# Norm gain moved from the activations to the first weights, and one kept product moved to another buffer

## The chip, the core and the metric

The program runs on one core of one Trainium2 chip. Five engines of the core appear in the profile: TensorE (PE, with its weight loads as PEld), VectorE (DVE), ScalarE (ACT), GpSimd (POOL) and SyncE (SP, which here only issues DMAs). Each executes its own instructions in order and waits on semaphores for the others. The metric is device time in microseconds (us) of one execution, the median of several runs. Lower is better.

## What is computed

Eight batches of attention with squared ReLU in place of softmax, 12 heads, 448 tokens and 64 columns a head, followed by a normalised two-layer block with a residual:

```python
scores = scale * np.matmul(q, k.transpose(0, 1, 3, 2))
attn = np.maximum(scores, 0.0) ** 2 / S
x = np.matmul(attn, v)                       # heads side by side: (8, 448, 768)
mu = np.mean(x, axis=-1, keepdims=True)
var = np.mean((x - mu) ** 2, axis=-1, keepdims=True)
xn = (x - mu) / np.sqrt(var + 1e-06) * g_ln
ch = np.maximum(xn @ w_ch1, 0.0) @ w_ch2     # 768 -> 3072 -> 768
out = x + ch
```

The vector g_ln has one number for each of the 768 columns of x, which are the rows of w_ch1. The division by the square root is left to the very end, since ReLU lets a positive factor of a token pass through.

## The kernel before

Batches are taken in pairs ("units"). A batch goes through these steps. Attention: `att_QK` writes scores into one of three PSUM slots (L610), `relu` evacuates them on ACT or DVE (L619, L621), `square` follows on DVE or POOL (L634, L636), and `att_AV` (L676) gives x transposed, columns of the model on partitions. `sum_part` adds the pieces of x on POOL into the fp32 buffer `sum_t` (L767, L769, L770). `center` multiplies that by ones on PE (L861), ACT saves the mean into `sum_t` again (`save`, L874), DVE subtracts it (`sub`, L882, four instructions) into the bf16 tile `xc`, and then `gain` multiplies `xc` by g_ln, in six instructions of 128x448, one for each 128 columns, each on ACT (L889) or DVE (L891). The first product reads `xc` and the weights `w1`, [128, 6, 3072] in bf16.

The first product has two forms. Batches 0 to 2 use plain matmuls (`ffn_1`, L971), six to a tile of 128 hidden columns, evacuated by `h_evac` (L1000 on ACT, L1002 on DVE) from two PSUM banks that take turns. From batch 3 on some groups of four tiles are computed with seven half-size products in place of eight (`ffn_1_product`, L1194). The other tiles of these batches stay plain, partly between the products in a slot of attention (`ffn_1_slot`, L989). The seven are called P1, P2, P6, P5, P7, P3, P4, in this order, on an "x" and a "y" bank. Three of their results are kept as fp32 copies outside PSUM (`keep`, L385 on ACT or L387 on DVE): c1 after P1, c2 after P6, p5 after P5. P7 goes on in the x bank and so waits until c2 has been copied. Another three results are added to a kept one by `add_relu` (L1220): C11 uses c1, C22 uses p5, C12 uses c2. Up to batch 6 the kept copies lie in the two buffers of `o_all`: c2 in the one that the last finished output tile was stored from, c1 and p5 in the other, so that each waits for the store of that buffer (`o_done`). In batch 7 they have buffers of their own.

The second product has the plain form (`ffn_2`, L1524) for five tiles of unit 0 and for one tile of each later unit, and a seven-product form (`ffn_w`, L1433) for the rest. In the plain form an output tile is two halves of 24 matmuls. Each half fills one of the two PSUM banks and is evacuated by one DVE instruction (L1540), which also multiplies by the token's factor from `rstd` (root on ACT, L838, reciprocal on DVE, L840) and adds x. A half needs the bank of the half two before it.

The order on every engine is fixed when the program is recorded: a planner (`Order`) keeps a modelled time for each engine, takes the ready operation that could start first, and writes it out. `R.add(engines, costs, emit, deps, key)` hands it an operation that may run on any of the named engines, and the key breaks ties. `segment` lays the matmuls of attention of the next batch ("visits") between those of the block, and runs "hooks" at given steps. `later(...)` and `now_known(...)` pass on an operation that is not yet recorded when another already needs it. POOL also issues the loads of q, k and v (L423, L442) as DMAs.

The stage that follows the first product of batch 1 matters for one of the edits. Its code is:

```python
segment(f1_steps(1) + f2_steps(0, (4, 5, 6, 3, 2)) + fw_steps(0, [0]), vis, 2, 9000.0,
        hooks=[(K2 // 2, lambda: make_sums(0))] ...
```

Of the kernel before, what the change touches and what calls it, by code (L numbers as in the profile page):

```python
# [202 lines left out]
def kernel(  # L203
# [10 lines left out]
    nc = tc.nc  # L214
# [535 lines left out]
    def sum_part(n):  # L750

        b, pn = divmod(n, NPER)
        if b < 2:
            parts = [(slice(0, S), [xT_of(b)[:, i, :] for i in (pn, pn + NPER)])]
        else:
            t, t_left = xT_of(b)
            parts = [(reg(b), [t[:, :, i, :] for i in (pn, pn + NPER)]),
                     (left(b), [t_left[:, i, :] for i in (pn, pn + NPER)])]
        k = 1 if pn == 0 else 2
        op = ops["x_read", b - 1] if pn == 0 else [ops["sum", n - 1]]  # L760
        for cols, x in parts:
            def add(eng, x=x, cols=cols):
                x0, x1, s0, r_t = *x, sum_t[:, cols], rsum_t[:, cols]
                if len(x0.shape) == 3:
                    s0, r_t = (a.rearrange("p (m c) -> p m c", c=P) for a in (s0, r_t))
                if pn == 0:
                    nc.gpsimd.tensor_add(s0, x0, x1)  # L767
                else:
                    nc.gpsimd.tensor_add(s0, s0, x0)  # L769
                    nc.gpsimd.tensor_add(s0 if pn < SUMMED[b] - 1 else r_t, s0, x1)  # L770
            w = cols.stop - cols.start
            ops["sum", n] = R.add("POOL", (120.0 + 2.03 * w) * k, add, ops["x", n] + op, key=-2.0, port=True)
            op = [ops["sum", n]]
# [76 lines left out]
    def center(b):  # L850
# [44 lines left out]
        if b < 2:  # L895
            for ki in [pn + NPER * h for pn in range(NPER) for h in range(2)]:
                def sub_k(eng, ki=ki):
                    if ki == 0:
                        alloc()
                    nc.vector.tensor_sub(xc[b][:, ki, :], xT_of(b)[:, ki, :], mean_ps[b])  # L900
                s1 = R.add("DVE", 620.0, sub_k, [op], key=-2.0)
                subs.append(s1)
                c_ops.append(R.add(*GAIN_ON, lambda eng, ki=ki: gain(eng, ki), [s1], key=-2.5, port=True))
        else:
            t, t_left = xT_of(b)
            for m in range(4):
                cols = slice(r0 + m * P, r0 + (m + 1) * P) if m < 3 else left(b)
                i = t[:, m] if m < 3 else t_left
                subs.append(R.add("DVE", 130.0 + (P if m < 3 else T) * K1 * 1.04,
                                  lambda eng, cols=cols, i=i: sub(eng, cols, slice(0, K1), i), [sv], key=-2.0))  # L910
            for ki in range(K1):
                c_ops.append(R.add(*GAIN_ON, lambda eng, ki=ki: gain(eng, ki), subs, key=-2.5, port=True))
        if b == 0:
            mean_ps["slot"][:] = [subs[-1]]
        elif b == 1:
# [107 lines left out]
    def h_of(b, a, z):  # L1023
        return [later("h", b, i) for i in range(a, z)]

    LAST_B = B - 1
    G4 = K2 // 4
    SH = S // 2
# [13 lines left out]
    def make_w1_sums(first):  # L1042
# [13 lines left out]
        def add(g, name, where):  # L1056

            def emit(eng):
                a11, a12, a21, a22 = (w1_block(g, r, h) for r in range(2) for h in range(2))
                if name == "S3":  # L1060
                    w1q[g, name] = a21
                    nc.vector.tensor_sub(a21, a11, a21)
                    return
                o = w1q[g, name] = home(*where[:2])
                if name == "S1":
                    nc.vector.tensor_add(o, a21, a22)
                elif name == "S2":
                    nc.vector.tensor_sub(o, w1q[g, "S1"], a11)
                else:
                    nc.vector.tensor_sub(o, a12, w1q[g, "S2"])  # L1070
            deps = list(where[2]) if where else [later("f1_end", b_done)]
            prev = {"S1": None, "S2": "S1", "S4": "S2", "S3": "S1"}[name]
            if prev:
                deps.append(ops["w1q", g, prev])
            ops["w1q", g, name] = R.add("DVE", 520.0, emit, deps, key=6.0, port=True)
# [95 lines left out]
    def ffn_1_product(b, g, name):  # L1171
# [32 lines left out]

        def kept(key):
            if b < LAST_B:
                t = o_all[:, e["o"] if key == "c2" else 1 - e["o"], :S]
            elif key == "c2":
                o = W_BLOCK + 3 * KQ * SH + (g % FLIGHT) * 2 * S
                t = at_all[:, o:o + 2 * S].bitcast(fp32)  # L1210
# [7 lines left out]
        def add_relu(key, row, half, other):  # L1218
            def emit(eng):
                nc.vector._custom_dve(TENSOR_ADD_SAT, out=h_out(row, half), in0=e["ps", bank], in1=kept(other),  # L1220
                                      s0=float("inf"), s1=0.0)
            e[key] = R.add("DVE", 620.0, emit, [op, e[other]], key=-3.0)

        def keep(key):
            def emit(eng):
                copy(eng, kept(key), e["ps", bank])
            free = [later("av_done", b)] if b == LAST_B else o_done[e["o"] if key == "c2" else 1 - e["o"]]
            e[key] = R.add(*EITHER, emit, [op, *free], key=-3.0)
        if name in ("P1", "P6", "P5"):
            keep({"P1": "c1", "P6": "c2", "P5": "p5"}[name])  # L1230
# [512 lines left out]
    with tc.manual_schedule():  # L1743
# [54 lines left out]
        def first_pair():  # L1798
# [1 line left out]
            pair_start(0, 0)  # L1800
        segment(f1_steps(1) + f2_steps(0, (4, 5, 6, 3, 2)) + fw_steps(0, [0]), vis, 2, 9000.0,
                hooks=[(K2 // 2, lambda: make_sums(0))]
                + [(i, next_sum) for i in range(K2 // 2 + 1, K2 + 6 * PARTS, SUM_EVERY)] + [(K2 + 6 * PARTS, lambda: make_sums(1)),
                       (K2 + 8 * PARTS, first_pair)]
                + [(i, next_sum) for i in range(K2 + 6 * PARTS + 1, K2 + 10 * PARTS + 2)])
        for b in range(2, B):
# [61 lines left out]
```

## Time and profile before

Three runs took 518.58, 518.02 and 517.56 us, median 518.02. The profiled execution took 518.0 us as a run, and its span in the trace, first instruction to last, is 516.1 us. The other 1.9 us lie around the span.

| what | in the profile before |
|---|---|
| PE busy | 500.2 us, 97% of the span |
| DVE busy | 397.5 us, 77% |
| ACT busy | 225.4 us, 44% |
| POOL busy | 178.3 us, 35% |
| granted TensorE clock | 1.00 in every stretch of 10 us up to 510 us |
| gain on DVE, L891, 128x448 | 30 instructions, 11.9 us |
| gain on ACT, L889, 128x448 | 18 instructions, 11.0 us |
| subtraction of the mean, L882 | 24 instructions, 20.1 us |
| kept products into `o_all`, L385 and L387 | 28 on ACT, 536 ns each; 8 on DVE, 619 ns each |

The first three batches' boundaries lie near 33 us (first product of batch 0 begins), 62 us (batch 1), 159.7 us (batch 2); batch 3's first product begins at 221 us, batch 5's at 342 us. In a timeline each row gives start, length, engine, line, operation, result and operands with their shape, and in brackets how long the engine had been idle before and what released it. Neighbouring instructions of one kind are merged into a row with a count.

### The profile page before, as it was taken

Reading aid. Unit: us, or ns where it says so; the run is one execution under the profiler, and the core shown is the slowest. Engines: PE = TensorE matmul, PEld = TensorE weight load, DVE = VectorE, ACT = ScalarE, POOL = GpSimd, SP = SyncE. Lnnn points to the kernel's source line nnn. Section 1 sums busy time; section 2 is a strip of 40 time slices with the busy share of each in tenths; the row PEclk is TensorE's granted clock in tenths of the full one; section 3 lists DMA queues with packets and bytes.
Section 4 is the critical chain, followed back from the end, with each engine's and each line's share of the span. In section 5 each row is a group of like instructions: output and inputs, shape, how many; then the busy total and the mean of one; then the engine's idle time right before and its main releaser. Section 6 shows DMA issues by size and latency. Waiting matters only on the chain.

```text
span 516.1 us, 10774 instructions
## 1 busy us (share of the span) xinstructions
PE 500.2 (97%) x4416; PEld 305.8 (59%) x4416; DVE 397.5 (77%) x751; ACT 225.4 (44%) x356; POOL 178.3 (35%) x205
## 2 busy tenths in 40 slices
PE   4899999999999999999999999999999999999997
PEld 3444455555554545667556775567655675579864
DVE  5988647847978879778778698885889688976843
ACT  5977622422303564255541565236641476125300
POOL 7420500425633066427543076232266023200000
PEclk9999999999999999999999999999999999999999
DMA  9999999789998178598288676894779620123022
GB/s 192 195 187 196 199 198 144 72 110 111 106 139 102 36 72 89 116 142 86 36 108 104 114 70 67 124 127 56 71 79 142 114 35 1 46 60 50 2 62 61
DMA packets 145948, 51.88 MB, mean 101 GB/s; under 512 B 123238, under 2 KB 144108, under 8 KB 145900
## 3 DMA queue, kind: packets, MB, share of 16 engines
q0 software_dynamic: 82224, 25.50, 46.8%
q1 hardware_dynamic: 59036, 18.82, 21.9%
q10 hardware_dynamic: 4640, 6.88, 4.6%
q8 instruction: 34, 0.56, 0.4%
q14 instruction: 14, 0.11, 0.1%
HBM read 51.91 MB, written 11.01 MB: 122 GB/s over the span
## 4 chain that ended last, share of the span: by engine, by line
PE 91%; DVE 5%; DMA 2%; ACT 1%; issue 1%; DVEq 0%; ACTq 0%
PE f_ps L1433 25%; PE f_ps L971 19%; PE f_ps L1524 12%; PE f_ps L1194 10%; PE sc L610 7%; PE ps L989 6%; PE ps L676 6%; PE x_ps L1194 2%; PE y_ps L1194 2%; DVE at_all L634 1%; DMA out_dram<-o_all 1%; DVE t L387 1%; DMA f<-in_q_dram 1%; DVE a L891 1%; ACT at_all L619 1%
## 5 line engine op out<-in xcount | busy, mean ns | idle before, releaser
L619 ACT ACTIVATE at_all<-sc 128x896 bf16<-128x896 f32 x120 | 105.4, 924 | 78.8 <-PE sc L610 75.8
L971 PE MATMUL f_ps<-a,w 128*128 128x448 bf16 x516 | 102.0, 353 | 1.2 <-DVE h L1002 0.8
L634 DVE TENSOR_TENSOR at_all<-at_all 128x896 bf16<-128x896 bf16 x154 | 96.8, 660 | 1.9 <-ACT at_all L619 1.9
L1433 PEld LDWEIGHTS <-h 128*128 128x128 bf16 x708 | 68.4, 98 | 47.3 <-issue 2.8
L442 POOL DMA_DIRECT2D v_t<-in_v_dram x36 | 21.5, 604 | 168.1 <-PE sc L610 147.5
L971 PEld LDWEIGHTS <-w 128*128 128x128 bf16 x516 | 48.9, 98 | 50.5 <-issue 7.5
L1433 PE MATMUL f_ps<-w,h 128*128 128x384 bf16 x360 | 62.8, 326 | 0.0
L423 POOL DMA_DIRECT2D t<-in_k_dram x36 | 55.9, 2132 | 0.0
L423 POOL DMA_DIRECT2D t<-in_q_dram x36 | 42.1, 1344 | 38.1 <-DMA t<-t 26.7
L621 DVE TENSOR_SCALAR at_all<-sc 128x896 bf16<-128x896 f32 x39 | 42.4, 1088 | 15.7 <-PE ps L676 8.7
L1000 ACT ACTIVATE h<-f_ps 128x448 bf16<-128x448 f32 (+1 forms) x65 | 32.9, 507 | 47.6 <-PE f_ps L971 46.2
L610 PE MATMUL sc<-t 64*64 64x448 bf16 x672 | 48.9, 364 | 3.2 <-ACT at_all L619 1.6
L1194 PEld LDWEIGHTS <-w 128*128 128x128 bf16 x432 | 41.0, 98 | 7.7 <-issue 4.7
L989 PE MATMUL ps<-a,w 128*128 128x448 bf16 x186 | 40.2, 352 | 0.0
L1524 PE MATMUL f_ps<-w,h 128*128 128x384 bf16 x240 | 40.0, 326 | 0.0
L1220 DVE CUSTOM_DVE_ANT_0 h<-f_ps,o_all 128x448 bf16<-128x448 f32 x36 | 21.8, 619 | 21.3 <-PE f_ps L1194 12.6
L610 PEld LDWEIGHTS <-t 64*64 64x64 bf16 x672 | 18.3, 106 | 26.1 <-issue 17.5
L1524 PEld LDWEIGHTS <-h 128*128 128x128 bf16 x240 | 23.3, 98 | 15.8 <-issue 0.6
L1194 PEld LDWEIGHTS <-t 128*128 128x128 bf16 x318 | 30.2, 98 | 4.1 <-issue 1.3
L1441 DVE SCALAR_TENSOR_TENSOR o_all<-f_ps,r_t,x_all 128x384 f32<-128x384 f32 x39 | 23.9, 613 | 11.0 <-PE f_ps L1433 10.8
L385 ACT CAST xT_all<-ps 128x768 bf16<-128x768 f32 (+2 forms) x28 | 17.8, 641 | 28.7 <-PE ps L676 17.7
L676 PE MATMUL ps<-at_all,v_t 64*64 64x448 bf16 x552 | 29.8, 350 | 0.0
(156 smaller groups left out, 712.4 us busy)
## 6 DMA issues: line engine op xcount, KB each, us to landing
w<-in_moe_w_ch_dram POOLq DMA_DIRECT2D x4, 1152.0 KB, 38.5
out_dram<-o_all ACTq DMA_DIRECT2D x43, 96.0 KB, 2.9
t<-in_q_dram POOLq DMA_DIRECT2D x36, 112.0 KB, 4.0
t<-in_k_dram POOLq DMA_DIRECT2D x36, 112.0 KB, 5.1
v_t<-in_v_dram POOLq DMA_DIRECT2D x36, 112.0 KB, 3.2
out_dram<-o_all SPq DMA_DIRECT2D x35, 96.0 KB, 2.2
w<-in_moe_w_ch_dram POOLq DMA_DIRECT2D x4, 768.0 KB, 18.9
out_dram<-o_all ACTq DMA_DIRECT2D x13, 192.0 KB, 3.1
```

Source lines behind the costliest of these rows:

```text
L423: nc.gpsimd.dma_start(qk_stage()[half * T:(half + 1) * T, t].rearrange("p j (h d) -> p j h d", d=D), src[b, h0:h0 + 2].rearrange("h (p j) ...
L610: nc.tensor.matmul(sc[rows_of(half), r, :S], turned[rows_of(r), 1, s, rows_of(half)], turned[rows_of(r), 0, :, rows_of(half)], start=True, ...
L619: nc.scalar.activation(attn[n, s], st[0][:, :, :S], Act.Relu, scale=rc2)
L621: nc.vector.tensor_scalar(attn[n, s], st[0][:, :, :S], rc2, 0.0, op0=Alu.mult, op1=Alu.max)
L634: nc.vector.tensor_mul(attn[n, s], attn[n, s], attn[n, s])
L676: nc.tensor.matmul(av_st[n][half][rows_of(hh)], (v_slot(n)[rows_of(half), hh] if b > 1 else vt[b][rows_of(half), 2 * pn + hh])[:, s * D:(s ...
L971: nc.tensor.matmul(st[0], w1[:, ki, ni * P:(ni + 1) * P], xc[b][:, ki, :], start=(i == 0), stop=(i == K1 - 1))
L989: nc.tensor.matmul(st[0], w1[:, ki, ni * P:(ni + 1) * P], xc[b][:, ki, :], start=ki == 0, stop=ki == K1 - 1)
L1000: nc.scalar.activation(o, st[0][:, c], Act.Relu)
L1194: nc.tensor.matmul(e["ps", bank][:, n, :], a[:, k, n * P:(n + 1) * P], x[:, k, :], start=name in ("P1", "P2", "P5") and n == 0 and k == 0, ...
L1433: nc.tensor.matmul(e["ps", bank], a(k), w(k), start=new and k == 0, stop=k == KH - 1, skip_group_check=True)
L1524: nc.tensor.matmul(o_st["ps"], stat(u, m, ki), w2[:, ki, j * hd:(j + 1) * hd], start=(ki == 0), stop=(ki == K2 - 1))
```

## The change

Two edits. First, `center` no longer multiplies `xc` by g_ln for batches 2 to 7. Instead a new function, `put_gains_on_w1`, multiplies `w1` itself by g_ln, in place, after the last first-product matmul of batch 1 (`f1_end`): twelve instructions of 128x1536, six row blocks in two halves, each on ACT or DVE by the planner's choice, called by a hook at the step where the second product of the first unit begins. Batches 0 and 1 keep their gain on x. The sums of weight blocks for the seven-product form now wait for the scaled weights. Second, in batches 3 to 6 the kept product c2 of the first group goes into `sum_t`, the buffer of the running sum and the mean, in place of `o_all`. It no longer waits for a store, and the first sum of the next batch on POOL, which writes `sum_t`, now waits for C12 of that group.

```diff
@@ sum_part
-        op = ops["x_read", b - 1] if pn == 0 else [ops["sum", n - 1]]
+        op = ops["x_read", b - 1] + [later("c2 read", b - 1) if 3 <= b - 1 < LAST_B else None] if pn == 0 else [ops["sum", n - 1]]
@@ center, b >= 2
-            for ki in range(K1):
-                c_ops.append(R.add(*GAIN_ON, lambda eng, ki=ki: gain(eng, ki), subs, key=-2.5, port=True))
+            c_ops = subs
@@ new
+    def put_gains_on_w1():
+
+        n = 2
+        for part in range(n):
+            cols = slice(part * d_ff // n, (part + 1) * d_ff // n)
+            done = []
+            for ki in range(K1):
+                def scale(eng, ki=ki, cols=cols):
+                    o = w1[:, ki, cols]
+                    if eng == "ACT":
+                        nc.scalar.mul(o, o, g_sb[:, ki:ki + 1])
+                    else:
+                        nc.vector.tensor_scalar(o, o, g_sb[:, ki:ki + 1], None, op0=Alu.mult)
+                done.append(R.add(("ACT", "DVE"), (1480.0, 500.0), scale, [ops["f1_end", 1]], key=2.0 + part))
+            for ni in range(part * K2 // n, (part + 1) * K2 // n):
+                ops["w1", ni] = done
@@ make_w1_sums
-            deps = list(where[2]) if where else [later("f1_end", b_done)]
+            deps = (list(where[2]) if where else [later("f1_end", b_done)]) + [ops["w1", 4 * g + 3]]
@@ ffn_1_product, kept
-                t = o_all[:, e["o"] if key == "c2" else 1 - e["o"], :S]
+                t = sum_t if key == "c2" and g == 0 else o_all[:, e["o"] if key == "c2" else 1 - e["o"], :S]
@@ add_relu
+            if key == "C12" and g == 0:
+                now_known(e[key], "c2 read", b)
@@ keep
-            free = [later("av_done", b)] if b == LAST_B else o_done[e["o"] if key == "c2" else 1 - e["o"]]
+            free = ([later("av_done", b)] if b == LAST_B else [] if key == "c2" and g == 0
+                    else o_done[e["o"] if key == "c2" else 1 - e["o"]])
@@ hooks of the segment shown above
-                + [(i, next_sum) for i in range(K2 // 2 + 1, K2 + 6 * PARTS, SUM_EVERY)] + [(K2 + 6 * PARTS, lambda: make_sums(1)),
+                + [(i, next_sum) for i in range(K2 // 2 + 1, K2 + 6 * PARTS, SUM_EVERY)] + [(K2, put_gains_on_w1), (K2 + 6 * PARTS, lambda: make_sums(1)),
```

Since the planner is asked again for the whole program, the recorded order may move elsewhere too. Recorded, it is as follows. PE issues the same matmuls in the same order, except that the mean matmul of batch 2 (L861) stands six matmuls of L1433 earlier. DVE loses 25 of its 30 L891 and gains eight scalings of 128x1536. ACT loses 11 of its 18 L889 and gains four scalings. The copy of c2 of the first group stands on ACT in all four batches; before, it stood on DVE (L387) in one of them, batch 3, and in batch 5 p5 of that group, which stood on DVE, is now on ACT as well. On POOL, in the sum of batch 2 near 146 us, one of two v loads (L442) stands ahead of two additions (L769, L770) instead of behind them. SP's order is the same. The eight scalings on DVE stand like this, L1540 being the evacuations of the first halves of the plain second product: reciprocal L840, one scaling, L1540, L634, L1540, L634, seven scalings, L1540. On ACT two scalings stand ahead of five L619 and the root L838, and two more after the next two L619, with two stores between them.

## The prediction

> **What bounds the kernel now.** I read the page's first two parts, then PE's waits, then timelines at the few places where PE stands still.
>
> ```profile
> PE 500.2 (97%) x4416; PEld 305.8 (59%) x4416; DVE 397.5 (77%) x751; ACT 225.4 (44%) x356; POOL 178.3 (35%) x205
> PE f_ps L532 <- DVE t L387: 4.8, 1, 4.8
> ...
> PE f_ps L1194 <- DVE o_all L387: 0.9, 1, 0.9
> PE f_ps L971 <- DVE h L1002: 0.8, 1, 0.8
> PE f_ps L1194 <- ACT o_all L385: 0.6, 1, 0.6
> ```
>
> PE is the bound, and the order of its matmuls hardly changes. So time is to be won only where PE waits, and is lost only where a new wait reaches it; busy time taken off DVE or ACT counts for nothing by itself. Most of PE's idle time is the first load and the first 30 us, which neither edit touches. Three places are left, each beside an edited operation. PE's timeline there, then DVE's, POOL's and ACT's:
>
> ```profile
> 159.71 1.12 PE L971 MATMUL f_ps<-a,w 128*128 128x448 bf16 x5
> 161.09 0.35 PE L971 MATMUL f_ps<-a,w 128*128 128x448 bf16 x1 [0.26 <-DVE a L891]
> 161.61 1.29 PE L971 MATMUL f_ps<-a,w 128*128 128x448 bf16 x6 [0.17 <-DVE o_all L1441]
> 163.67 2.62 PE L971 MATMUL f_ps<-a,w 128*128 128x448 bf16 x13 [0.77 <-DVE h L1002]
> ...
> 224.46 1.30 PE L989 MATMUL ps<-a,w 128*128 128x448 bf16 x6
> 226.63 0.73 PE L1194 MATMUL f_ps<-t,w 128*128 128x224 bf16 x6 [0.87 <-DVE o_all L387]
> ```
> ```profile
> 157.89 3.14 DVE L891 TENSOR_SCALAR a<-a,g_sb 128x448 bf16<-128x448 bf16 x4
> 160.96 0.60 DVE L1441 SCALAR_TENSOR_TENSOR o_all<-f_ps,r_t,x_all 128x384 f32<-128x384 f32 x1
> ...
> 225.95 0.62 DVE L387 COPY o_all<-f_ps 128x448 f32<-128x448 f32 x1 [1.25 <-DMA out_dram<-o_all]
> ...
> 455.76 1.07 DVE L891 TENSOR_SCALAR a<-a,g_sb 128x448 bf16<-128x448 bf16 x4
> ```
> ```profile
> 157.41 2.35 POOL L423 DMA_DIRECT2D t<-in_q_dram  x2 [6.98 <-DMA t<-t]
> 159.06 3.05 POOL L423 DMA_DIRECT2D t<-in_k_dram  x2
> ```
>
> The bracketed idle times understate a wait, since ends of matmuls are modelled; I count by starts. Thirteen matmuls in 2.62 us, the last 0.35 long, start every (2.62 - 0.35)/12 = 0.189 us. From 159.71 the sixth was due at 159.71 + 5 x 0.189 = 160.66 and came at 161.09: 0.43 late. The next was due at 161.28, came at 161.61: 0.33. Six later, due 162.74, came 163.67: 0.93. Together 1.69 us at batch 2. At batch 3, P7 was due at 224.46 + 6 x 0.189 = 225.59 and came at 226.63: 1.04. At batch 5 the same sum gives 347.31 - (345.39 + 1.13) = 0.79, released by the copy of c2 on ACT at 346.73. In all **3.52 us**.
>
> **Removed: the gain on x.** At batch 2 four L891 take 3.14 us, at batch 7 the same four 1.07. The difference is POOL: at 157 it issues the loads of q and k. Single L891s there, of 331 ns median, ended 0.09 to 0.16 us after the end of a POOL issue (for instance 158.59 to 159.91, POOL's to 159.76). Behind them on DVE stand L1441, which frees a bank (161.56), then the relu L621, then L1002. That is all three waits of batch 2. Without them, L1441 follows the end of its matmuls at 159.1 and ends at 159.7; L621 (1.08) ends at 160.7, L634 (0.61, after ACT's L619 to 160.4) at 161.25, L1002 at 161.8. The second tile's end, where PE asks for that bank, is 159.71 + 12 x 0.189 = 161.98. ACT's L1000 for the next tile comes behind two store issues (1.12) and an L619, and ends at about 162.9 against 163.1. Both fit, with 0.2 us to spare; I take the whole **-1.69**, and -0.8 as the other end, if the 0.93 stays. At batches 3 to 7 the gains are under 48 matmuls of the second product (7.96 us at 212.43) and PE showed no wait for them: nothing.
>
> **Moved: c2 of the first group.** At batch 3 its copy L387 waited until 225.95 for a store issued at 221.08 (the chain has 4.75 us of DMA there). In `sum_t` it waits for P6 alone: six matmuls of 0.096 after 223.31, so 223.9; ACT's L1000 before it ends at 224.11, the copy (536 ns) at 224.65, ahead of 225.59. At batch 5 the copy would end near 345.5, ahead of 346.52. So **-1.04** and **-0.79**. Next late could be p5 in the other buffer, behind c2 on ACT: it ends at 225.2, and P3 needs it at 226.2. The other end is 0 for each, if a store not in this list holds the copy. At batches 4 and 6 the trace shows no such wait: nothing. The new wait of POOL's first sum for C12: at batch 3 C12 is done at 228.66 and the sum starts at 232.58, held by an evacuation; 3.9 us of cover, and behind it on POOL only loads.
>
> **Added: twelve scalings of w1.** No row has one. ACT: SBUF rows of 128x448 (L889, 660 ns) and 128x896 (L632, 1004) give 0.77 ns a column and 1.50 us for 1536; with 1.04 ns a column it would be 1.79. The first two run from 96.9, after the last L1000, and end at 99.9 to 100.4. The three L619 behind, at 99.61 before, slip by 0.3 to 0.8. Their slots are asked for at 101.93 and 103.51; the tightest, freed at 103.28 and used at 103.72, allows 0.4. I take nothing, at most 0.4. The other two ACT scalings have 8.42 us idle behind them, up to 114.31.
>
> DVE: L1504 (256 columns 483 ns, 128 columns 351) has about 0.22 fixed. L891's 0.331 less this is 0.11 for 448 columns, so 0.22 + 0.11 x 1536/448 = 0.60 us, 0.63 with L1441's fixed part (613 ns for 384, 343 for 128: 0.21). If nothing of L891 were fixed, 1.14. I take 0.63. Where they stand matters:
>
> ```profile
> 104.02 9.92 PE L1524 MATMUL f_ps<-w,t 128*128 128x384 bf16 x60
> ...
> 104.66 0.17 DVE L840 RECIPROCAL r_t<-r_t 128x4 f32<-128x4 f32 x1
> 104.95 0.62 DVE L1540 SCALAR_TENSOR_TENSOR o_all<-f_ps,r_t,x_all 128x384 f32<-128x384 f32 x1
> 105.48 1.15 DVE L634 TENSOR_TENSOR at_all<-at_all 128x896 bf16<-128x896 bf16 x2
> 106.55 0.61 DVE L1540 SCALAR_TENSOR_TENSOR o_all<-f_ps,r_t,x_all 128x384 f32<-128x384 f32 x1
> 110.08 0.62 DVE L1540 SCALAR_TENSOR_TENSOR o_all<-f_ps,r_t,x_all 128x384 f32<-128x384 f32 x1 [2.91 <-PE f_ps L1524]
> ...
> 103.73 3.13 POOL L423 DMA_DIRECT2D t<-in_k_dram  x2
> ```
>
> One scaling stands between the reciprocal and the first L1540. L1524 has 18 matmuls at 96.16, 12 at 99.87 and 6 at 102.43 before these 60, so at 104.02 the second half of 24 lacks twelve, and the third half starts at 104.02 + 12 x 0.163 = 105.98, in the bank that this L1540 frees at 105.57. Handing over takes 0.06 (225.95 + 0.62 to 226.63), so there is 0.35 of cover. Alone, the scaling delays by 0.63 - 0.09 of overlap = 0.54: a stall of 0.2. But POOL is issuing k (single issues 103.73 to 105.69 and 104.50 to 106.86). Held as the L891s were, the scaling ends when the first issue ends, plus 0.1 and the rest of its columns, 0.3: 106.1. L1540 then ends at 106.65, PE goes on at 106.7: **+0.72**. Held to the second issue's end it is 107.3, L1540 at 107.8, a stall of 1.9. I take 0.72, by the row that is nearest: an L891 ran in 317 ns at 159.83, inside an issue, just after the one before had ended at 159.76.
>
> The Trainium skill (SBUF — State Buffer, Who interferes with whom) says that a VectorE instruction in a two-port mode and a GpSimd operation lock each other out: the first gets the shared ports for its whole length, and the other stands still. It lists the multiplication by a scalar among the kinds that can do so. By that rule both issues, which began before the scaling, hold it, the stall is 1.9 and the time 516.4. The 317 ns row speaks against so strict a reading.
>
> The other seven start at 108.3, after L634, with POOL idle from 106.9 to 116. They take 7 x 0.54 = 3.8 us and end at 112.1; L1540 behind them ends at 112.7. The half that wants this bank starts at 116.15, after visits: 3.4 us of cover.
>
> **Sum.** -1.69 - 1.04 - 0.79 + 0.72 = -2.80. On the profiled execution, 518.0 (span 516.1 and 1.9 around it), that is 515.2. The median is 518.02, so the same. With the ends: from 518.0 - 3.52 + 0.2 = 514.7, or 514.3 with 0.3 us of a bank wait at 231.21 to 231.61 that may go too and a little of the runs' scatter, to 518.0 - 3.52 + 1.9 = 516.4.
>
> **Rivals.** (a) A gain is taken by another wait: 0.93 of batch 2 stays, its slack being 0.2 us, or a store still holds c2 once. For: L1000 and L1002 stand in queues with three things ahead. Against: each of these is released by PE itself. With 0.93 kept, 516.1; with both c2 gains lost, 517.0; with the 0.93 and the long first stall, 517.3. (b) The waits are hidden anyway, and the change does not do in time what it says: PE, released earlier, waits as long for the next bank. For: every wait here is a bank or a copy in a chain. Against: none of the three is followed by a second wait before the next boundary. 518.0. (c) Slower: the scalings do not run at L891's rate. At L1504's rate, 1.03 ns a column, one takes 1.8 us. The first then stalls PE by 1.8 - 0.09 - 0.35 = 1.4. The seven end at 109.5 + 7 x 1.7 = 121.4, L1540 behind them at 122.0, when PE wants the bank at 117.5: 4.5 more. 518.0 - 3.52 + 5.9 = 520.4. With t for one, the two stalls are t - 0.44 and, from t = 1.15, 7t - 8.05; they eat the 3.52 at t = 1.5 us. For: POOL held single L891s to 1.32. Against: the same type and kind as L891, and POOL is idle under the seven.
>
> **How the numbers follow.** Forecast 0.66, (a) 0.16, (b) 0.10, (c) 0.08. A measurement can tell about 0.2% from no change, 1.04 us: below 516.98 is faster. That has the forecast and three quarters of (a): 0.78. Same is (b) and the rest of (a): 0.14. Slower is (c): 0.08. The range 514.3 to 517.3 holds the forecast and (a), and leaves out (b) and (c). The forecast's own range is 514.3 to 516.5.
>
> **What would show it.** PE's first-product rows at batch 2 without gaps; P7 right after L989 at batches 3 and 5; one new gap of about 0.7 us in L1524 near 106; scalings of some 0.63 us on DVE, the first one longer, and 1.5 to 1.8 on ACT. It is wrong if a scaling takes over 1.5 us, if the gap near 106 is above 2, or if PE waits for another evacuation at batch 2 or for a store at batch 3.

## The result, and the profile after

The changed kernel takes **515.42 us** in the median (514.68 to 517.06, 17 runs). The kernel before, run beside it, takes 518.68 us (517.25 to 521.57, 17 runs). The ratio is 0.994, with a 95% interval of 0.9927 to 0.9953. The forecast was 515.2 us, in a range of 514.3 to 517.3. The profiled execution took 515.06 us with a span of 513.2 us, against a span of 516.1 us before: 2.9 us less.

First the busy times of the page of the changed kernel:

```profile
PE 500.2 (97%) x4416; PEld 305.9 (60%) x4416; DVE 389.9 (76%) x732; ACT 225.6 (44%) x351; POOL 177.7 (35%) x205
```

PE has the same 500.2 us of work. DVE has lost 7.6 us of it, and the span 2.9. The two numbers have little to do with each other, as the experiments show. Then the longest and the newest of PE's waits after the change:

```profile
PE f_ps L532 <- DVE t L387: 4.9, 1, 4.9
...
PE sc L610 <- DVE at_all L621: 0.2, 1, 0.2
```

The columns are the tile and line that waited, what it waited for, the sum, the count and the longest wait, in us. The first load stands as before. The three waits at 160 to 164, and those of P7 at batch 3 and at batch 5, are gone from the list, and one of 0.2 us is new. In the new source the lines have moved: L970 is L971 of before, L988 is L989, L999 and L1001 are L1000 and L1002, L1210 is L1194, L1236 is L1220, L1452 and L1460 are L1433 and L1441, L1543 and L1559 are L1524 and L1540. The scalings are L1035 (ACT) and L1037 (DVE). PE's timeline at the places of the prediction:

```profile
104.05 10.18 PE L1543 MATMUL f_ps<-w,t 128*128 128x384 bf16 x60
...
160.00 5.85 PE L970 MATMUL f_ps<-a,w 128*128 128x448 bf16 x30
...
223.07 1.30 PE L988 MATMUL ps<-a,w 128*128 128x448 bf16 x6
224.20 0.74 PE L1210 MATMUL f_ps<-t,w 128*128 128x224 bf16 x6
...
354.44 0.38 PE L610 MATMUL sc<-t 64*64 64x448 bf16 x4 [0.15 <-DVE at_all L621]
```

The first thirty matmuls of batch 2, which stood in four stretches, have become one with no hole: (5.85 - 0.35)/29 is 0.190 us a matmul. P7 (224.20) follows L988 after 1.13 us, which is six matmuls of 0.189. The sixty matmuls at 104.05 take 10.18 us where they took 9.92. And at 354.44 a scores product waits for a slot for which it did not wait before.

The sum can be made exactly. PE issues the same 4416 matmuls in the same order, but for the mean matmul of batch 2, so each can be laid beside itself in the other trace. Where the difference of the starts makes a step, time was won or lost there. The steps are, with the times of before:

| place | predicted, us | measured, us |
|---|---|---|
| second product, third half, at 106 | +0.72 | +0.26 |
| batch 2, three waits | -1.69 | -0.42, -0.33, -0.93: -1.68 |
| batch 3, P7 | -1.04 | -1.04 |
| batch 5, P7 | -0.79 | -0.79 |
| scores at 357 (354 after) | 0 | +0.28 |
| sum | -2.80 | -2.97 |

The spans differ by 2.9; under 0.1 us lies in the start and the end. Below, "steps" are always read in this way. The medians differ by 3.26 us; the kernel before has 518.68 beside the changed one, 0.66 more than in the three runs that the forecast started from (518.02).

### The profile page after: what moved, and what is told of

Same layout as the page of the kernel before. It is cut to its first block, busy times and chain, and to the rows that moved or that the text cites. A ratio compares the mean times of both kernels' runs of the same rounds, so it can differ in the third digit from the quotient of the medians.

```text
span 513.2 us, 10746 instructions
## 1 busy us (share of the span) xinstructions
PE 500.2 (97%) x4416; PEld 305.9 (60%) x4416; DVE 389.9 (76%) x732; ACT 225.6 (44%) x351; POOL 177.7 (35%) x205
## 4 chain that ended last, share of the span: by engine, by line
PE 94%; DVE 3%; ACT 1%; DMA 1%; issue 1%; ACTq 0%; DVEq 0%
PE f_ps L1452 26%; PE f_ps L970 19%; PE f_ps L1543 12%; PE f_ps L1210 10%; PE ps L988 7%; PE sc L610 7%; PE ps L676 5%; PE x_ps L1210 2%; PE y_ps L1210 2%; DVE at_all L634 1%; ACT at_all L619 1%; DVE t L387 1%; DMA f<-in_q_dram 1%; PE ps L532 1%; PE f_ps L950 0%
## 5 line engine op out<-in xcount | busy, mean ns | idle before, releaser
L619 ACT ACTIVATE at_all<-sc 128x896 bf16<-128x896 f32 x120 | 105.4, 925 | 101.1 <-PE sc L610 99.8
L970 PE MATMUL f_ps<-a,w 128*128 128x448 bf16 x516 | 101.5, 353 | 0.0
L634 DVE TENSOR_TENSOR at_all<-at_all 128x896 bf16<-128x896 bf16 x154 | 96.8, 660 | 1.9 <-ACT at_all L619 1.9
L1452 PEld LDWEIGHTS <-h 128*128 128x128 bf16 x708 | 68.4, 98 | 47.3 <-issue 2.8
L442 POOL DMA_DIRECT2D v_t<-in_v_dram x36 | 21.5, 603 | 170.2 <-PE sc L610 145.1
L970 PEld LDWEIGHTS <-w 128*128 128x128 bf16 x516 | 48.9, 98 | 48.8 <-issue 5.5
L1452 PE MATMUL f_ps<-w,h 128*128 128x384 bf16 x360 | 62.8, 326 | 0.0
L621 DVE TENSOR_SCALAR at_all<-sc 128x896 bf16<-128x896 f32 x39 | 42.4, 1087 | 15.9 <-PE ps L676 8.7
L999 ACT ACTIVATE h<-f_ps 128x448 bf16<-128x448 f32 (+1 forms) x65 | 32.9, 506 | 47.6 <-PE f_ps L970 46.3
L1210 PEld LDWEIGHTS <-w 128*128 128x128 bf16 x432 | 41.0, 98 | 5.8 <-issue 2.7
L988 PE MATMUL ps<-a,w 128*128 128x448 bf16 x186 | 40.2, 352 | 0.0
L1543 PE MATMUL f_ps<-w,h 128*128 128x384 bf16 x240 | 40.0, 326 | 0.0
L1236 DVE CUSTOM_DVE_ANT_0 h<-f_ps,o_all 128x448 bf16<-128x448 f32 x32 | 19.5, 619 | 20.3 <-ACT h L999 6.9
L1460 DVE SCALAR_TENSOR_TENSOR o_all<-f_ps,r_t,x_all 128x384 f32<-128x384 f32 x39 | 23.9, 613 | 12.0 <-PE f_ps L1452 11.9
L1543 PEld LDWEIGHTS <-h 128*128 128x128 bf16 x240 | 23.3, 98 | 15.8 <-issue 0.6
L1210 PEld LDWEIGHTS <-t 128*128 128x128 bf16 x318 | 30.2, 98 | 4.1 <-issue 1.3
L1460 DVE SCALAR_TENSOR_TENSOR o_all<-f_ps,r_t,o_all 128x384 f32<-128x384 f32 x30 | 18.4, 614 | 16.5 <-PE f_ps L1452 16.5
```

What stands on the lines that cost most here:

```text
L619: nc.scalar.activation(attn[n, s], st[0][:, :, :S], Act.Relu, scale=rc2)
L621: nc.vector.tensor_scalar(attn[n, s], st[0][:, :, :S], rc2, 0.0, op0=Alu.mult, op1=Alu.max)
L634: nc.vector.tensor_mul(attn[n, s], attn[n, s], attn[n, s])
L970: nc.tensor.matmul(st[0], w1[:, ki, ni * P:(ni + 1) * P], xc[b][:, ki, :], start=(i == 0), stop=(i == K1 - 1))
L988: nc.tensor.matmul(st[0], w1[:, ki, ni * P:(ni + 1) * P], xc[b][:, ki, :], start=ki == 0, stop=ki == K1 - 1)
L999: nc.scalar.activation(o, st[0][:, c], Act.Relu)
```

## The experiments

The theory: the 1.69 us at batch 2 are the price of the gain on x, held by POOL, and nothing else; the 1.83 us of P7 are the price of c2 waiting for a store; the gains of batches 3 to 7 are worth nothing; the first scaling costs what POOL holds it; the other seven are under cover. The rivals: batch 2 gained because a mean matmul moved up; the two edits each bring their part without the other; the removed busy time itself brings time.

| kernel | span, us | median, us (runs) | ratio to before, 95% interval |
|---|---|---|---|
| c2 edit alone | 514.6 | 516.22 (10) | 0.995 (0.9931 to 0.9969) |
| gain edit alone | 516.0 | 517.26 (10) | 0.997 (0.9949 to 0.999) |
| before, no gain at batch 2 | 515.1 | 517.20 (10) | 0.9975 (0.9952 to 0.9997) |
| before, no gain at batches 3 to 7 | 516.8 | 518.85 (10) | 0.9994 (0.9975 to 1.0014) |
| changed, scalings later | 513.2 | 514.77 (8) | 0.9933 (0.991 to 0.9956) |
| changed, seven scalings tripled | 522.3 | 523.16 (5) | 1.0082 (1.0051 to 1.0113) |
| gain edit alone, small load at batch 3 | 515.0 | 516.93 (10) | 0.9966 (0.9949 to 0.9984) |
| changed, small load at 102 | 513.4 | 515.23 (5) | 0.9932 (0.9906 to 0.9959) |
| changed, first scaling tripled | 515.4 | 517.23 (1) | one run, no interval |
| scalings later, two more writes | 512.6 | 514.69 (6) | 0.9932 (0.9917 to 0.9948) |
| scalings later, one more write | 512.6 | 514.41 (1) | one run, no interval |

A span is that of one traced execution, and these differ in the first 35 us, which no edit touches: against the trace of before PE is late there by 0.81 us in the gain edit alone, 0.56 in the changed kernel with the small load at 102, 0.88 with seven scalings tripled, 0.35 with the first one tripled, 0.32 with the scalings later, 0.15 in the gain edit with the small load at batch 3, and under 0.05 in the others. So spans should not be compared by themselves. The steps below are those behind the first 35 us, unless a place is given. Each kernel has its own line numbers.

### The two edits apart

The second edit alone: the gain stays on x, and `put_gains_on_w1` and its uses are out.

```diff
-            c_ops = subs
+            for ki in range(K1):
+                c_ops.append(R.add(*GAIN_ON, lambda eng, ki=ki: gain(eng, ki), subs, key=-2.5, port=True))
...
-    def put_gains_on_w1():
...
```

> The second edit alone: c2 of the first group into sum_t, the gain still on x. My theory: P7 at batches 3 and 5 no longer waits for a store, 1.04 and 0.79 us, so 1.8 us below the kernel before (0.4%), or 1.5 if the new wait of 0.28 us at the scores near 354 us in the changed kernel is a price of this edit. That wait then shows here too, and the three late starts at batch 2 (0.43, 0.33, 0.93) stay. Rival: PE is released earlier only to wait as long for the next bank or store, no change within 0.5 us. Rival on the 0.28: it belongs to the missing gain, and does not show here.

The steps are -1.04 and -0.79 at the two P7, as in the changed kernel, and the step at 354 is not there. But there are two others beside P7 of batch 3, +0.23 and +0.30 at 221 to 224, and -0.19 at batch 2, where POOL's issues begin 0.19 us earlier (157.22 for 157.41) and the last gain held by them ends 0.19 us earlier: net -1.48. The cause of the two is in the timelines of DVE and of POOL before these waits:

```profile
216.87 2.06 DVE L891 TENSOR_SCALAR a<-a,g_sb 128x448 bf16<-128x448 bf16 x2
```
```profile
216.43 2.34 POOL L423 DMA_DIRECT2D t<-in_q_dram  x2 [5.91 <-DMA t<-t]
```

In the kernel before, POOL's issue began at 217.32, and the same two gains took 0.57 us at 217.06. Here it begins 0.9 us earlier, meets them, and they take 2.06. DVE's relu L621 behind them starts at 221.49, not at 220.96. So the gain at batch 3 had a price that did not show, because POOL came just after it.

The first edit alone: c2 stays in `o_all`.

```diff
-                t = sum_t if key == "c2" and g == 0 else o_all[:, e["o"] if key == "c2" else 1 - e["o"], :S]
+                t = o_all[:, e["o"] if key == "c2" else 1 - e["o"], :S]
...
```

> The first edit alone: twelve scalings of w1, no gain on x in batches 2 to 7, c2 back in its output buffer. My theory: the 1.69 us at batch 2 go, the stall near 106 us stays (0.26 in the changed kernel's profile, up to 0.7 by where POOL's issues fall), the waits of 1.04 and 0.79 at P7 come back: 1.0 to 1.4 us below the kernel before. Rival: with gains gone at batches 3 and 5 the boundary is earlier and P7's wait for the store changes in size, by up to 0.5 us either way. If both edits are independent, this and the other edit alone sum to the changed kernel's gain, 2.9 us of span.

Batch 2 gives its whole 1.68 us, the first scaling costs 0.10, and then P7 of batch 3 takes 0.74 back: net -0.86 (the span shows next to nothing of it, because this trace was 0.81 us late at the start). In PE's timeline and in the chain of waits of this kernel:

```profile
223.69 1.30 PE L988 MATMUL ps<-a,w 128*128 128x448 bf16 x6
226.61 0.73 PE L1210 MATMUL f_ps<-t,w 128*128 128x224 bf16 x6 [1.62 <-DVE o_all L387]
```
```profile
220.31 5.50 DMA out_dram<-o_all
```

P7 was due at 223.69 + 1.13 = 224.82 and came 1.79 late, where before it was 1.04. The store was issued 0.77 us earlier than before (220.31 for 221.08) and landed at the same time: 5.50 us after its issue in place of 4.75. What PE wins at batch 2 it waits for at the store. Thus the edits do not add up: -1.48 and -0.86 make -2.34, and the two together give -2.97. Together they are rid of the 0.74 at the store and of the 0.52 of the held gains, and pay 0.19 at batch 2 that both had counted, 0.15 more at 106 and the new 0.28: -2.34 - 1.26 + 0.62 = -2.98.

### The gain at one batch and at the others

```diff
             for ki in range(K1):
-                c_ops.append(R.add(*GAIN_ON, lambda eng, ki=ki: gain(eng, ki), subs, key=-2.5, port=True))
+                if b != 2:
+                    c_ops.append(R.add(*GAIN_ON, lambda eng, ki=ki: gain(eng, ki), subs, key=-2.5, port=True))
+            c_ops = c_ops or subs
```

> The kernel before with the gain left out for batch 2 alone and no scaling of w1: batch 2's first product is computed without g_ln. My theory: all of the gain edit's worth is here, 1.69 us below the kernel before, with no late start among the first matmuls of batch 2. Rival: a part of it comes from the planner moving the mean matmul of batch 2 six matmuls forward, which this kernel does not do; then 0.3 to 1 us of waits stay at batch 2.

Steps: -0.42, -0.33 and -0.93 at batch 2, and +0.60 at P7 of batch 3, where the store is again waited for. So the gains at batch 2 are the whole price there. The opposite kernel has `if b == 2`:

> The kernel before with the gain left out for batches 3 to 7 and no scaling of w1: their first product is computed without g_ln; batch 2 keeps its gain. 20 instructions less on DVE and 10 on ACT, some 14 us of busy time. My theory: these were under 48 matmuls of the second product, so the time is that of the kernel before within 0.3 us, with the same PE waits. Rival: DVE at 77% is a second bound, and taking 14 us of it and ACT off shortens the run by 1 us or more.

Some fourteen microseconds less of busy time on DVE and ACT bring nothing; the median is the same within the interval, and the steps are -0.47 at batch 2, where POOL's issues begin 0.47 us earlier (156.94 for 157.41) and the last gain again ends with them, +0.98 at P7 of batch 3 and +0.30 near 357. PE's timeline and the chain at P7:

```profile
223.98 1.30 PE L991 MATMUL ps<-a,w 128*128 128x448 bf16 x6
227.13 0.73 PE L1196 MATMUL f_ps<-t,w 128*128 128x224 bf16 x6 [1.85 <-DVE o_all L387]
```
```profile
220.60 5.74 DMA out_dram<-o_all
```

P7 is 227.13 - (223.98 + 1.13) = 2.02 late, and the store takes 5.74 us. It is issued half a microsecond before its time in the kernel before, and lands half a microsecond after. POOL's loads start earlier too (at 216.70 for 217.32), and their packets may stand in front of the store's. The next kernel asks whether they are to blame: the first edit alone, and the q and k loads of the pair that is fetched there cut to one of seven blocks.

```diff
+                    js = slice(0, 1 if n in (14,) else J)
-                        qk_stage()[half * T:(half + 1) * T, t].rearrange("p j (h d) -> p j h d", d=D),
+                        qk_stage()[half * T:(half + 1) * T, t, js].rearrange("p j (h d) -> p j h d", d=D),
...
```

> The kernel with the first edit alone, c2 in its output buffer, with the loads of q and k for one pair of heads (issued by POOL near 216 us, as the second product before batch 3 ends) cut to one seventh of their rows; that pair's attention is computed partly on old rows. In the run of the first edit alone P7 at batch 3 waited 1.78 us for a store, 0.74 more than in the kernel before. My theory: the store's 128 packets share the 16 DMA engines with the 3584 packets of 128 bytes of these loads, so with 512 of them the store lands some 3 us after its issue in place of 5.5, and the wait of 1.78 at P7 goes: 1.3 to 1.8 us less than the first edit alone. Rival: the store waits for a fixed time, or for the transposes on the other queue, and the wait stays above 1 us.

The store lands 4.62 us after its issue at 220.17 in place of 5.50, and P7's step is 0.88 us smaller than in the first edit alone. So the loads cost P7 0.88 us, by these two traces; the medians, 517.26 and 516.93, do not tell the two kernels apart. That is less than the 1.3 to 1.8 us expected: P7 still comes 0.91 us late. What the rest of the 4.62 us is stays open; the other half of the tile is stored by SP at that time, and SP's transposing loads run then too, and neither was tried.

### The first scaling

Only ten of the twelve scalings are made to wait, until the first half has been evacuated; this puts the first DVE scaling behind the evacuations. The first two scalings, on ACT, stay where they were.

```diff
-                done.append(R.add(("ACT", "DVE"), (1480.0, 500.0), scale, [ops["f1_end", 1]], key=2.0 + part))
+                done.append(R.add(("ACT", "DVE"), (1480.0, 500.0), scale,
+                                  [ops["f1_end", 1]] + ([later("first half out")] if (part, ki) > (0, 1) else []), key=2.0 + part))
...
+        if (u, m, j) == (0, 4, 0):
+            now_known(ev, "first half out")
```

> The changed kernel, with ten of the twelve scalings held back until the first half of the second product has been evacuated, so that none stands ahead of that evacuation on DVE. My theory: the stall of PE near 106 us goes, 0.26 us of span, up to 0.7 by where POOL's issues fall; all else as in the changed kernel: 514.8 to 515.4 us. Rival: the delay comes from the two scalings on ACT, which hold up the relu and the root, not from the one on DVE; then the stall stays.

Against the changed kernel there is -0.26 at 106 and +0.23 at 31.7, a place that no edit touches and where the last two kernels below, with the same order there, show no such step. The stall at 106 is gone: the sixty matmuls take 9.93 us. The two scalings on ACT still stand ahead of the relu and the root (97.17, 3.04 us), so the rival falls.

The changed kernel with the loads of the pair that is fetched at 102 cut to one of seven blocks (the edit above with `n in (8,)`):

> The changed kernel with the loads of q and k for one pair of heads (issued by POOL near 102 to 106.5 us) cut to one seventh of their rows; that pair's attention is computed partly on old rows. In the changed kernel the first scaling on DVE took 0.91 us, the other seven 0.53 from start to start. My theory: it was held by POOL's issue of k until that ended. With short issues it takes about 0.61, the evacuation behind it ends at 105.9, and the stall of 0.26 us at 106.1 shrinks to 0.1 or nothing. Rival: the 0.91 is the price of a first scaling, in any case, and stays.

The first scaling and its neighbours on DVE, and POOL's issue of k, in this kernel, which runs 0.53 us behind the changed one here:

```profile
105.23 0.17 DVE L841 RECIPROCAL r_t<-r_t 128x4 f32<-128x4 f32 x1
105.31 0.59 DVE L1038 TENSOR_SCALAR w<-w,g_sb 128x1536 bf16<-128x1536 bf16 x1
105.82 0.61 DVE L1560 SCALAR_TENSOR_TENSOR o_all<-f_ps,r_t,x_all 128x384 f32<-128x384 f32 x1
```
```profile
103.41 1.22 POOL L424 DMA_DIRECT2D t<-in_k_dram  x2
```

POOL is done at 104.63, the scaling takes 0.59 us in place of 0.91, and the step at 106 against the changed kernel is -0.26: no stall is left. So all of the 0.26 is POOL's hold, and the scaling unheld is wholly under the two free banks; the 0.2 us that the prediction gave it was too much. The rows say why: the evacuation starts 105.82 - 105.23 = 0.59 us after the reciprocal starts, where it was 104.95 - 104.66 = 0.29 before. The scaling delays it by 0.30 us, not by 0.54, because it begins in the time that the evacuation had to wait behind the reciprocal anyway. That is less than the cover of 0.35. How long is the hold? The changed kernel, DVE and then POOL's first issue of k:

```profile
104.70 0.17 DVE L840 RECIPROCAL r_t<-r_t 128x4 f32<-128x4 f32 x1
104.78 0.91 DVE L1037 TENSOR_SCALAR w<-w,g_sb 128x1536 bf16<-128x1536 bf16 x1
105.61 0.60 DVE L1559 SCALAR_TENSOR_TENSOR o_all<-f_ps,r_t,x_all 128x384 f32<-128x384 f32 x1
...
107.73 3.78 DVE L1037 TENSOR_SCALAR w<-w,g_sb 128x1536 bf16<-128x1536 bf16 x7
111.43 0.60 DVE L1559 SCALAR_TENSOR_TENSOR o_all<-f_ps,r_t,x_all 128x384 f32<-128x384 f32 x1
114.27 0.62 DVE L1559 SCALAR_TENSOR_TENSOR o_all<-f_ps,r_t,x_all 128x384 f32<-128x384 f32 x1 [2.23 <-PE f_ps L1543]
```
```profile
103.35 1.96 POOL L423 DMA_DIRECT2D t<-in_k_dram  x1
```

The issue ends at 103.35 + 1.96 = 105.31, and the scaling at 105.69, 0.38 later. Three other kernels have this scaling in the same place, with POOL's issue falling elsewhere. The scaling ends at 106.32, 106.78 and 106.17, the issue that was running at 105.94, 106.39 and 105.79: 0.38 to 0.39 us each. The steps at 106 against the kernel before are +0.10 (gain edit alone), +0.49 (seven tripled, below) and +0.61 (gain edit with the small load at batch 3, whose load at 102 is whole). So the price goes by where the issue falls, and the 0.72 predicted is not far out of this spread. The next kernel has the first DVE scaling followed by two more multiplications:

```diff
+                        scaled[0] += 1
+                        for _ in range(2 if scaled[0] == 1 else 0):
+                            nc.vector.tensor_scalar(o, o, 1.0, None, op0=Alu.mult)
```

> The changed kernel with the first VectorE scaling alone followed by two multiplications of its result by 1.0 (the value is not changed). Two questions. What a microsecond in front of the first evacuation costs: that scaling stands ahead of the first evacuation of the unit's second product and has two free banks behind it; if it is paid one to one beyond what is already waited for (0.26 us at 106), the two added multiplications, 0.53 us each from start to start, add 1.06 us there. If there were still cover, less. And what the 0.28 us at 354 is: in every run so far that shows it, the same VectorE instruction starts 0.45 us after its semaphore event in place of 0.10, and it is the 575th event of VectorE (577th, 584th, 585th or 589th in the runs that don't). If it goes by the place in VectorE's instruction stream, two more instructions move it and the step at 354 is gone: span 513.2 + 1.06 - 0.28 = 514.0. If it goes by what else runs at that time, the order there is the same and the step stays: 514.3.

The step at 106 is +2.21 us against the changed kernel, not 1.06. DVE and PE in this kernel (L1041 is the added multiplication):

```profile
105.10 0.78 DVE L1038 TENSOR_SCALAR w<-w,g_sb 128x1536 bf16<-128x1536 bf16 x1
105.92 1.14 DVE L1041 TENSOR_SCALAR w<-w 128x1536 bf16<-128x1536 bf16 x1
...
108.15 0.60 DVE L1563 SCALAR_TENSOR_TENSOR o_all<-f_ps,r_t,x_all 128x384 f32<-128x384 f32 x1
```
```profile
108.80 3.41 PE L1547 MATMUL f_ps<-w,t 128*128 128x384 bf16 x20 [2.30 <-DVE o_all L1563]
```

Each of the three is held by another of POOL's issues. These end at 105.50, 106.67 and 107.84, and the three end at 105.88, 107.06 and 108.23: 0.38 to 0.39 us after each. So the added microsecond cost twice what it costs unheld. The second question of this run is answered below.

### The cover of the other seven

```diff
+                        scaled[0] += 1
+                        for _ in range(2 if scaled[0] > 1 else 0):
+                            nc.vector.tensor_scalar(o, o, 1.0, None, op0=Alu.mult)
```

> The changed kernel, with the last seven DVE scalings each followed by two multiplications of the same weights by 1.0: 14 more instructions of 128x1536, about 7.4 us of DVE. The forecast gave the seven 3.4 us of cover, up to the bank that the fifth half needs; by that the end at 119.5 us meets a need at 116.4, and the time rises by 3.0 us over the changed kernel. My theory now: the cover is smaller, since a relu of scores (L621) stands behind the evacuations and PE needs its slot at about 116; it would end near 121, so PE loses about 5 us: 520 to 521 us. Rival: DVE is idle for 2 us there and catches up later, 1 us or less.

The span is 9.1 us longer than the changed kernel's. From the first of the seven to the evacuation behind them DVE takes 120.84 - 108.81 = 12.03 us, where it took 111.43 - 107.73 = 3.70: 8.33 added. DVE's timeline and PE's of the tripled kernel:

```profile
120.84 1.14 DVE L1563 SCALAR_TENSOR_TENSOR o_all<-f_ps,r_t,x_all 128x384 f32<-128x384 f32 x2
121.89 1.08 DVE L621 TENSOR_SCALAR at_all<-sc 128x896 bf16<-128x896 f32 x1
```
```profile
123.03 0.59 PE L610 MATMUL sc<-t 64*64 64x448 bf16 x4 [5.70 <-DVE at_all L621]
```

PE does not wait for the bank of the evacuation L1563, which the prediction had looked at, but for a scores slot that the relu L621 behind it frees. The step there is 5.83 us. So the cover was 8.33 - 5.83 = 2.5 us; 2.23 of it is the idle time of DVE ahead of L1559 at 114.27, in the timeline of the changed kernel above. The prediction had 3.4. A further 2.5 us were lost behind the wait, and these are no wait at all. (0.23 at 106, where POOL held the first scaling longer, and 0.85 in the first 35 us make up the rest, less the 0.28 at 354, which is gone here: 5.83 + 2.5 + 0.23 + 0.85 - 0.28 = 9.1.) The 520 to 521 us expected left out these 2.5. Busy time by stretch in the tripled kernel (PE, PEld, DVE, ACT, POOL, each with its count, then the granted clock, the DMA share and GB/s):

```profile
117.00:123.00 6.00, 0.32 (x8) 0.07 (x1) 5.86 (x11) 0.00 (x0) 1.30 (x2) 0.88 0.28 38
123.00:125.00 2.00, 1.97 (x9) 0.85 (x9) 2.00 (x4) 1.62 (x2) 0.40 (x1) 0.50 0.77 197
125.00:128.00 3.00, 3.00 (x17) 1.19 (x18) 1.63 (x4) 0.00 (x0) 3.00 (x5) 0.50 0.02 3
128.00:135.00 7.00, 7.00 (x52) 3.94 (x45) 3.57 (x6) 1.73 (x2) 2.77 (x3) 0.97 1.04 68
```

After 5.70 us without a matmul the granted clock is 0.50 for some 5 us, and the matmuls there lose the 2.5 us, most of them 0.16 us each. The waits of 0.3 to 2.3 us in the other kernels had no such follow-up. The Trainium skill (TensorE: Matmul & The Clock Gate, Part 1: The HAM clock gate) says that the clock falls to half after at least one idle window of about 3.4 us and comes back after at least one busy window of about that length; the rows agree with the half, and a return after some 5 us of matmuls does not contradict it.

### The new wait at 354

Two traces with the same instructions around the place help here. The changed kernel's DVE, and then that of the last but one kernel, whose edit is

```diff
-    nc.vector.memset(eps_sb, 1e-6)
+    for _ in range(3): nc.vector.memset(eps_sb, 1e-6)
```

> The version with ten of the twelve scalings held back until the first half's evacuation, and two more writes of the one-column constant eps at the start of VectorE's stream (the same value again, under 0.1 us of work, before any product). Nothing else moves. If the 0.28 us at 354 goes by the instruction's place in VectorE's stream, it is gone or elsewhere: span 513.2 - 0.28 = 512.9, and 514.5 us in the median. If it goes by what runs beside it, nothing changes: 513.2 and 514.8 us.

```profile
349.55 0.62 DVE L1236 CUSTOM_DVE_ANT_0 h<-f_ps,o_all 128x448 bf16<-128x448 f32 x1 [3.41 <-ACT h L999]
352.76 0.62 DVE L1236 CUSTOM_DVE_ANT_0 h<-f_ps,o_all 128x448 bf16<-128x448 f32 x1 [2.59 <-PE sc L610]
```
```profile
349.62 0.62 DVE L1237 CUSTOM_DVE_ANT_0 h<-f_ps,o_all 128x448 bf16<-128x448 f32 x1 [3.77 <-ACT h L999]
352.13 0.62 DVE L1237 CUSTOM_DVE_ANT_0 h<-f_ps,o_all 128x448 bf16<-128x448 f32 x1 [1.88 <-PE f_ps L1211]
```

In the changed kernel the first addition has 3.41 us idle ahead of it and the second 2.59. With two more writes in front of the whole program it is 3.77 and 1.88: the late start has moved by two events of DVE, to the addition before, where nobody waits, and the step at 354 is gone (-0.28). The trace has the events that this counts: the late instruction starts 0.45 us after its own semaphore event in place of 0.10, and is event 575 of DVE (counted from 0) in both.

> The same with one more write in place of two. By the place in the stream the late start moves to a neighbour of the instruction, one earlier in program order: gone from this line at 354, or on another instruction near it. By what runs beside it, it stays, with the span at 513.2.

With one more write (`range(2)`) event 575 is a semaphore event with 2.1 us idle ahead of it; no addition is late there and the step is gone too. The kernel with the first scaling tripled, with two more instructions, has lost it as well, and the one with seven tripled, with fourteen. All of the kernels that showed it (the changed one, the one without gains at batches 3 to 7, the later scalings, the small load at 102) have the same addition as event 575. So the 0.28 us is no price of either edit. It goes by the place of an instruction in DVE's stream, and not by that alone: in the gain edit alone an addition is event 575 too, but stands right behind another with no idle time between, and is not late. Why that place is late, no run shows.

The two versions with more writes are the fastest of all: 512.6 us of span, 514.69 us in the median of 6 runs. That is 0.6 us less span than the changed kernel, and its interval (0.9917 to 0.9948) overlaps that of the changed kernel (0.9927 to 0.9953), so by time alone the two are not told apart; by the traces the difference is the two steps, 0.26 and 0.28.

## Why the prediction was right

**Batch 2, P7 at batch 3, P7 at batch 5:** right to 0.01 us each, and by the causes given: without the gain on x the three waits go, in each kernel that leaves it out at batch 2 and wherever the mean matmul stands; with c2 in `sum_t` P7 follows L988 at once. The doubt that L1000 left only 0.2 us of slack at batch 2 did not come true.

**The first scaling:** the mechanism was right, the size not: 0.26 for 0.72. The scaling ended 0.38 us after the end of POOL's first issue; the prediction had put 0.4. But it took that issue's end, 105.69, from the trace of before, and in the changed kernel POOL began 0.38 us earlier (103.35 for 103.73), so the issue ended at 105.31. Most of the difference of 0.46 is this; the rest is 0.02 to 0.03 us each in the hold, in the evacuation behind it and in the time at which PE asks for the bank. The delay of 0.54 us by an unheld scaling was too large as well (0.30 by the small load); it did not enter the 0.72. The stall of 1.9 that the Trainium skill's rule gave (SBUF — State Buffer, Who interferes with whom) did not come: the scaling was held by the running issue to its end, as the rule says, but not by the next, whose record had begun before it. With the first scaling tripled the three in a row cost 2.21 + 0.26 = 2.5: each is held by one issue, and ends while the record of the next is open.

**The other seven:** nothing lost, as predicted, but with a cover of 2.5 us and not 3.4. The step that failed looked at the bank, asked for at 116.15, and not at the relu behind the evacuation, whose slot PE asks for first. The rival with dear scalings would have come earlier by this, at (2.5 + 3.0)/7 + 0.53 = 1.3 us for one scaling at the latest (an estimate, 3.0 being what the change won, without a longer first scaling and a lower clock), not at 1.5. The scalings take 0.53 us from start to start where 0.54 was expected, and those on ACT 1.57 to 1.59, within the 1.50 to 1.79.

**Nothing for the gains at batches 3 to 7:** right for this kernel as a term of the sum, and too simple as a reason. Without c2's edit, their going away ends in a longer wait for the store (+0.98), and with c2's edit alone they stay, and are met by POOL (+0.52). The terms of the sum were each measured against the schedule of before; the schedule that came moved POOL's issues beside batch 3 by 1.8 us and PE by 1.4, and with them the price of each.

**Not foreseen:** +0.28 at 354. It and the mis-sized stall have opposite signs, which is part of why 515.2 lies so near 515.42. The other part is scatter: the forecast was a fall of 2.80 us, the traces show 2.9 and the medians 3.26. That nearness is luck; the three large terms are not. The bank wait of 0.3 us at 231, put at the edge of the range, stayed (at 228.8 to 229.2).

## What to carry to other kernels

- Cost an edit at the waits of the bound engine, start by start; the 7.6 us of DVE work that went away are worth nothing of themselves, and the 1.68 us of waiting behind four instructions of them are all that their removal won.
- When two waits lie in a row, and the second is for a transfer that keeps its own time, winning the first is paid back at the second (+0.60, +0.74, +0.98 here) until both are removed; try the edits alone and together before judging either.
- A price that rests on two engines meeting is a matter of phase: look at it with the other engine moved by a microsecond either way, as the gains at batch 3 (0.57 us or 2.06 us for two) and the first scaling show.

## What the runs showed of the hardware

A VectorE multiplication of bf16 rows in SBUF that ran into a DMA issue of POOL ended a fixed time after that issue: 0.38 to 0.39 us for 1536 columns in seven cases from five kernels, 0.10 to 0.16 for 448 in most of the gains L891 that were held. The 0.285 us between 0.385 and 0.100 is 0.26 ns a column, as in the unheld ones (0.61 and 0.33 us); so it looks as if all of the data is moved behind the issue. The one that waits was not held by the next issue as well, whose record had already begun; the one behind it could be. Evacuations from PSUM (L1559, 0.60) and the squares L634 (0.61) beside the same issues were not longer.

A store of 64 packets of 3072 bytes (half a tile) that shares its time with loads of 128-byte packets landed 4.75 to 5.74 us after its issue, and 4.62 with most of these loads gone; issued 0.5 or 0.8 us earlier beside the whole loads, it landed no earlier.

In five kernels the addition that is event 575 of VectorE, behind an idle wait, started 0.35 us late; two writes of one column at the start moved the late start to another addition, where it costs nothing.
